# A fused attention and feed-forward kernel on one core: the first phase put in order by a list scheduler

## The chip, the core and the metric

The kernel runs on one core of a Trainium2 chip. The time is the device time of one execution in microseconds (us), from runs of the whole kernel. Five engines take part, each with a queue of its own that it works off in order: TensorE (PE, the matmuls, with the weight loads shown as PEld), VectorE (DVE), ScalarE (ACT), GpSimd (POOL, which does almost nothing here) and SyncE (SP), which issues every DMA. An instruction at the head of a queue waits on semaphores for what it reads, and everything behind it in that queue waits with it.

## The reference

Linear attention with a positive feature map, then a gated feed-forward block on its output:

```python
def phi(x):
    proj = np.einsum('bhsd,df->bhsf', x, w_phi)
    proj = proj - np.max(np.abs(proj), axis=-1, keepdims=True)
    return np.concatenate([np.exp(proj), np.exp(-proj)], axis=-1)
q_p, k_p = (phi(q), phi(k))
kv = np.einsum('bhsf,bhsd->bhfd', k_p, v)
z = np.sum(k_p, axis=2)
num = np.einsum('bhsf,bhfd->bhsd', q_p, kv)
den = np.einsum('bhsf,bhf->bhs', q_p, z)[..., None] + 1e-06
...
gate = 1.0 / (1.0 + np.exp(-(x @ w_gate)))
val = x @ w_val
return gate * val @ w_out
```

There are 8 batches, 8 heads, 576 positions of 64 numbers and 128 features. The feed-forward block ("FF") has 4608 tokens, a width of 512 and a hidden width of 1536, which is cut into 12 slices of 128.

## The kernel before

**Two phases.** The first phase does all of the attention and, between its pieces, the first 4 of the 12 FF slices (JA = 4), whose weights stay in on-chip memory. The second phase (`rest_chunks`) does the other 8 slices in blocks of 512 tokens and adds the partial result of the first phase. The change touches the first phase alone.

**An attention step** handles one pair of heads of one batch; there are 32, counted by i. On PE it has the key projection `pk` (16 matmul records for the two heads, into two PSUM banks, and a small one for the last 64 keys, `pk{i}_2`, into a third), the query projection `pq` in two halves of two banks each, the key-value product `kvz`, its transposition `tp`, the numerators `nm` (two halves) and the denominators `dp`. DVE takes the largest magnitude of the keys (`mx`), subtracts it (`dk`), and from step 10 on adds up the keys' exponentials (`s`, `su`), so that `kvz` has fewer matmuls; of the queries it takes the largest magnitude with transposing instructions (`pm`, `pn`, `mb`) and subtracts it (`d`). ACT does all exponentials (`ek`, `eq`, `d`) and copies out of PSUM. The denominators go through memory (`dn`, `den`, `rb`: three DMAs in a row with a reciprocal on DVE between the first and the second), and DVE multiplies: `xp`, the attention output, which is stored to `xs`. Batch 0 hands its output to the FF directly as well (`xh`, `xl`).

**An FF chunk** is 256 tokens; there are 18, counted by c. Each has 8 halves of 12 matmuls (`gv`: the gate and value products of the 4 slices) and two output blocks of 12 matmuls (`acc`). Behind each pair of halves stand two activations and a cast on ACT (`t`, `u`, `hh`) and four instructions on DVE (`t`, `t`, `u`, `hl`). Every value is kept as a high and a low part, which is why one product takes three matmuls. A chunk can start when the attention of its tokens is stored.

**Weights.** Each of the 12 weight tiles of the first phase is loaded twice (`wraw`, `wmid`) and turned from 64-bit numbers into the two parts by five DVE instructions (`weight_tile`). The second phase does the same (`from_f64`, six DVE instructions a tile) for 24 tiles; 14 of them lie in the last hundred microseconds of the first phase, when the attention's buffers have become free for them.

**The order** in the first phase is what the program text records (`manual_schedule`). The loop over i writes the PE pieces of neighbouring steps in a fixed sequence and calls `fill` four times a step. `fill` puts FF halves and output blocks (`ready`) behind them, at a rate that spreads the FF work of a batch over the steps until the next batch is due. Whatever hangs on a piece is a generator that `tick` moves on by one stage, so that its place on DVE and ACT follows from how many ticks have passed. PSUM banks of the attention come from one pool of 5 (`ps_a`); `gv` has 2 and `acc` 1. Nearly all attention buffers are held twice.

Of the kernel before, what the change touches and what calls it, by code (L numbers as in the profile page):

```python
# [20 lines left out]
F = 128  # L21
P = 128
# [16 lines left out]
RATE = 2.8  # L39
LAG = (4, 8)  # L40
AHEAD = 3
TICKS = 3
# [3 lines left out]
def attention_moe(  # L46
# [63 lines left out]
    def raw_tile(w, sp):  # L110

        j, m = divmod(w, 3)
        raw = sp.tile([P, 2 * DM], U32, tag="wraw", name=f"wraw{j}_{m}")
        nc.sync.dma_start(raw, w_moe[j, :, m, :].bitcast(U32))
        mid = sp.tile([P, 2 * DM], U32, tag="wmid", name=f"wmid{j}_{m}")
        nc.sync.dma_start(
            mid[:, : 2 * DM - 1].bitcast(U16),
            w_moe[j, :, m, :].bitcast(U16)[:, 1 : 4 * DM - 1],
        )
        return raw, mid  # L120

    def weight_tile(w, raw, mid, wp, sp):
        j, m = divmod(w, 3)
        n = f"{j}_{m}"
        if m == 0:
            weights[j] = tuple(
                wp.tile([P, 3 * DM], F32R, tag=f"w{x}{j}", name=f"w{x}{j}") for x in "hl"
            )
        h, l = (x[:, m * DM : m * DM + DM] for x in weights[j])
        hi = raw.rearrange("p (n two) -> p n two", two=2)[:, :, 1]  # L130
        words = mid.rearrange("p (n two) -> p n two", two=2)
        rest, unit = words[:, :, 0], words[:, :, 1]
        top = sp.tile([P, DM], U32, tag="wtop", name="wtop" + n)
        vec.tensor_scalar(top, hi, 0x7FFFFE00, None, op0=ALU.bitwise_and)
        act.activation(top, top, AF.Relu, bias=ebias, scale=8.0)
        vec.tensor_scalar(rest, rest, 0x01FFFFFF, None, op0=ALU.bitwise_and)
        yield
        vec.scalar_tensor_tensor(
            top, hi, 0x80000000, top, op0=ALU.bitwise_and, op1=ALU.bitwise_or
        )  # L140
        nc.sync.dma_start(h.bitcast(U32), top)
        yield
        vec.tensor_scalar(unit, top, 0xFF800000, None, op0=ALU.bitwise_and)
        vec.scalar_tensor_tensor(
            l, rest, 2.0**-36, unit.bitcast(F32), op0=ALU.mult, op1=ALU.mult
        )

# [40 lines left out]

    tasks = []

    def start(g):

        if next(g, tasks) is not tasks:
            tasks.append(g)

    def tick():
        for g in list(tasks):
            if next(g, tasks) is tasks:
                tasks.remove(g)

    def half_units(js, mp, ps_gv, ps_acc, need):
        xs, hs, gvs, parts = {}, {}, {}, collections.Counter()

        def load_x(c):
            xh, xl, raw = x_tiles(mp, CH, f"1_{c}")
            xs[c] = xh, xl
            nc.sync.dma_start(raw, xscr[c])
            for _ in range(3):
                yield
            act.copy(xh, raw)  # L210
            yield
            vec.tensor_tensor(xl, raw, xh.bitcast(F32), op=ALU.subtract)  # L212
            parts[c] = NP

        def begin(c):
            free = c < 2 or parts["v", c - 2] == len(js)
            if c not in xs and free and parts["x", c] == CH * NP:
                start(load_x(c))

        def gate(c, i, n):  # L220
            gv = gvs.pop((c, i))
            u = mp.tile([P, CH], F32, tag="u", name="u" + n)
            t = mp.tile([P, CH], F32, tag="t", name="t" + n)
            hh = mp.tile([P, CH], F32R, tag="hh", name="hh" + n, bufs=10)
            hl = mp.tile([P, CH], F32R, tag="hl", name="hl" + n, bufs=10)
            hs[c, i] = hh, hl, None
            act.activation(t, gv[:, 0, :], AF.Tanh, scale=0.5)
            act.activation(u, gv[:, 0, :], AF.Exp)
            yield
            tu = t.bitcast(U32)  # L230
            vec.tensor_scalar(tu, tu, 0x7FFFFFFF, None, op0=ALU.bitwise_and)
            vec.scalar_tensor_tensor(t, t, 1.0, gv[:, 1, :], op0=ALU.add, op1=ALU.mult)
            vec.scalar_tensor_tensor(u, u, 1.0, t, op0=ALU.min, op1=ALU.mult)
            yield
            act.copy(hh, u)  # L235
            yield
            vec.tensor_tensor(hl, u, hh.bitcast(F32), op=ALU.subtract)  # L237
            parts["h", c] += 1

        def half(c, i, m):  # L240
            while parts[c] < NP:
                begin(c)
                tick()
            need(js[i], m)
            n = f"1_{c}_{js[i]}"
            if m == 0:
                gvs[c, i] = ps_gv.tile([P, 2, CH], F32, tag="gv", name="gv" + n)
            mm_in(gvs[c, i][:, m, :], xs[c], js[i], m, CH)
            if m == 1:
                parts["v", c] += 1  # L250
                start(gate(c, i, n))
                begin(c + 1)

        def half_out(c, t):
            need(js[-1], 2)
            while parts["h", c] < len(js):
                tick()
            acc = ps_acc.tile([P, DM], F32, tag="acc", name=f"acc1_{c}_{t}")
            for i, j in enumerate(js):
                mm_out(acc, t, hs[c, i], j, i == 0, i == len(js) - 1)  # L260
            y = mp.tile([P, DM], F32, tag="y", name=f"y1_{c}_{t}")
            act.activation(y, acc, AF.Copy, scale=0.5)

            def store():
                yield
                nc.sync.dma_start(yscr[c][t], y)

            start(store())

        def unit(c, i):  # L270
            return [(1.45, lambda m=m: half(c, i, m)) for m in range(2)]

        def chunk(c):

            items = []
            for i in range(len(js)):
                items += unit(c, i)
                if i < 2:
                    items += outs(c - 1)[i : i + 1]
            return items  # L280

        def first():

            items = []
            for i in range(len(js)):
                items += unit(0, i) + unit(1, i)
            return items + outs(0)

        def outs(c):
            return [(0.69 * len(js), lambda t=t: half_out(c, t)) for t in range(2)]  # L290

        return chunk, first, outs, begin, xs, parts
# [60 lines left out]
    with ExitStack() as actx:  # L353
# [8 lines left out]

        steps = [(b, p) for b in range(B) for p in range(NP)]
        N = len(steps)

        def bank(shape, name, i=N, ps=None, tag=None):

            if i < EARLY:
                return ps.tile(shape, F32, tag=tag, name=name)
            return ps_a.tile(shape, F32, tag="a", name=name)  # L370
# [106 lines left out]
        def copies(cs):  # L477
            for o, x in cs:
                act.copy(o, x)
# [391 lines left out]
```

## Time and profile before

| | |
|---|---|
| three runs | 1291.21, 1295.24, 1296.06 us (median 1295.24) |
| span of the profiled execution, first to last instruction | 1291.7 us; the profile gives no other time for it |
| first phase, to the first matmul of the second | 694.8 us |
| last transposition of the attention (`tp31`) | 587.2 us |
| PE, DVE, ACT busy in the span | 96%, 61%, 41% |

The profile gives the busy time of each engine in any stretch, the clock that TensorE was granted there (PEclk, 1.00 is full), the single instructions in order of time, and for each idle time the instruction that ended it. Matmuls are pipelined: the time between the starts of two blocks says what a block costs, while a matmul's own duration is longer than that.

### The profile page before, as it was taken

How to read it: one execution, taken by the hardware profiler on the slowest of the kernel's cores; microseconds unless marked ns; L12 is line 12 of the kernel's file. 1: busy time of each engine (PE TensorE's matmuls, PEld its weight loads, DVE VectorE, ACT ScalarE, POOL GpSimd, SP SyncE). 2: the span in 40 equal slices, each digit the busy share in tenths (PEclk: the TensorE clock that was granted, in tenths of full speed). 3: DMA queues.
4: the chain of work that ended last, by engine and by line, in shares of the span. 5: the costliest groups of instructions: out<-in, count | busy, mean ns of one | idle time of the engine just before them, and what ended most of it. 6: DMA issues, size and time to landing. Idle time of an engine off the chain costs nothing.

```text
span 1291.7 us, 22705 instructions
## 1 busy us (share of the span) xinstructions
PE 1234.4 (96%) x9264; PEld 971.2 (75%) x9264; DVE 786.1 (61%) x1584; ACT 528.1 (41%) x1081; POOL 0.7 (0%) x6
## 2 busy tenths in 40 slices
PE   7767999999999999999889999999999999999998
PEld 5434677777777777777778888888888888888886
DVE  6779778888878778883895953434243434333333
ACT  4635556665655566563443422212222212222221
POOL 0000000000000000000000000000000000000000
PEclk8877899999999999999899999999999999999999
DMA  4448434343433334332754520202020111111010
GB/s 176 153 145 284 136 104 146 111 132 105 127 119 121 99 98 146 98 104 73 270 195 148 195 98 1 95 3 76 22 61 37 58 40 53 46 41 57 6 61 33
DMA packets 80868, 131.56 MB, mean 102 GB/s; under 512 B 18300, under 2 KB 37884, under 8 KB 80764
## 3 DMA queue, kind: packets, MB, share of 16 engines
q1 hardware_dynamic: 80764, 130.11, 31.4%
q8 instruction: 73, 1.20, 0.4%
q14 instruction: 31, 0.25, 0.1%
HBM read 92.04 MB, written 28.45 MB: 93 GB/s over the span
## 4 chain that ended last, share of the span: by engine, by line
PE 86%; DVE 7%; DMA 3%; ACT 2%; issue 1%; SPq 0%; DVEq 0%
PE acc L172 22%; PE g L165 15%; PE v L165 15%; PE gv L165 13%; PE kvz L534 6%; PE nm L584 4%; PE pq L417 3%; PE dp L597 2%; PE pk L427 2%; PE kvz L548 1%; DMA wraw<-w_moe 1%; PE pk L488 1%; ACT ek L460 1%; PE tp L560 1%; DMA rb<-den 1%
## 5 line engine op out<-in xcount | busy, mean ns | idle before, releaser
L165 PE MATMUL gv<-xh,wh 128*128 128x256 f32 x576 | 171.6, 298 | 4.9 <-ACT xh L210 2.6
L172 PE MATMUL acc<-wh,hh 128*128 128x512 f32 x432 | 172.4, 399 | 3.2 <-ACT hh L235 2.5
L172 PE MATMUL acc<-wh,hl 128*128 128x512 f32 x432 | 169.0, 391 | 0.7 <-DVE hl L237 0.7
L172 PE MATMUL acc<-wl,hh 128*128 128x512 f32 x432 | 169.1, 391 | 0.0
L165 PE MATMUL gv<-xl,wh 128*128 128x256 f32 x576 | 164.5, 286 | 2.8 <-DVE xl L212 2.8
L165 PE MATMUL gv<-xh,wl 128*128 128x256 f32 x576 | 164.3, 285 | 0.0
L63 ACT CAST hh<-u 128x512 fp32r<-128x512 f32 x72 | 44.7, 621 | 229.0 <-DVE u L186 229.0
L184 DVE TENSOR_SCALAR t<-t 128x512 uint32<-128x512 uint32 x72 | 30.7, 426 | 166.9 <-ACT t L181 166.7
L165 PEld LDWEIGHTS gv<-xh,wh 128*128 128x128 f32 x576 | 111.5, 194 | 22.7 <-issue 15.7
L181 ACT ACTIVATE t<-g 128x512 f32<-128x512 f32 x72 | 43.0, 598 | 178.5 <-PE g L165 178.4
L165 PEld LDWEIGHTS gv<-xl,wh 128*128 128x128 f32 x576 | 111.7, 194 | 3.5 <-DVE xl L212 3.0
L165 PE MATMUL g<-xh,wh 128*128 128x512 f32 x288 | 113.0, 392 | 0.0
L165 PE MATMUL v<-xh,wh 128*128 128x512 f32 x288 | 112.6, 391 | 0.0
L165 PE MATMUL g<-xh,wl 128*128 128x512 f32 x288 | 112.5, 391 | 0.0
L165 PE MATMUL g<-xl,wh 128*128 128x512 f32 x288 | 112.5, 391 | 0.0
L165 PE MATMUL v<-xl,wh 128*128 128x512 f32 x288 | 112.3, 390 | 0.0
L165 PE MATMUL v<-xh,wl 128*128 128x512 f32 x288 | 112.1, 389 | 0.0
L165 PEld LDWEIGHTS gv<-xh,wl 128*128 128x128 f32 x576 | 111.5, 194 | 0.0
L185 DVE SCALAR_TENSOR_TENSOR t<-t,v 128x512 f32<-128x512 f32 x72 | 49.4, 686 | 97.3 <-PE v L165 97.3
L172 PEld LDWEIGHTS acc<-wh,hh 128*128 128x128 f32 x432 | 81.1, 188 | 27.3 <-issue 6.2
L172 PEld LDWEIGHTS acc<-wh,hl 128*128 128x128 f32 x432 | 81.1, 188 | 20.2 <-DVE hl L237 1.7
L534 PE MATMUL kvz<-ek,v 128*32 128x256 f32 x1280 | 89.6, 433 | 6.8 <-issue 5.8
(97 smaller groups left out, 2141.1 us busy)
## 6 DMA issues: line engine op xcount, KB each, us to landing
wraw<-w_moe SPq DMA_DIRECT2D x36, 512.0 KB
xl<-xs SPq DMA_DIRECT2D x34, 512.0 KB
k<-k SPq DMA_DIRECT2D x32, 320.0 KB
v<-v SPq DMA_DIRECT2D x32, 320.0 KB
q<-q SPq DMA_DIRECT2D x32, 288.0 KB
wh<-wtop SPq DMA_DIRECT2D x36, 256.0 KB
ys<-y SPq DMA_DIRECT2D x36, 256.0 KB
yp<-ys SPq DMA_DIRECT2D x36, 256.0 KB
```

What stands on the lines that cost most here:

```text
L63: a = act.copy(h, x)
L165: nc.tensor.matmul(o, a[:, ws], x[:, cs], start=i == 0, stop=i == 11)
L172: nc.tensor.matmul(acc, a[:, ts], w[:, ws], start=first and i == 0, stop=last and i == 2)
L181: act.activation(t, g, AF.Tanh, scale=0.5)
L184: vec.tensor_scalar(tu, tu, 0x7FFFFFFF, None, op0=ALU.bitwise_and)
L185: vec.scalar_tensor_tensor(t, t, 1.0, vl, op0=ALU.add, op1=ALU.mult)
L417: nc.tensor.matmul(pps[hd], wk[head(hd), :], x[head(hd), cs], start=True, stop=True)
L427: nc.tensor.matmul(pps[hd][:, t, :], kx[head(hd), t * P : t * P + P], wk[head(hd), :], start=True, stop=True,)
L460: act.activation(e[:, :, sg * F : sg * F + F], dk, AF.Exp, scale=1.0 - 2.0 * sg)
L534: nc.tensor.matmul(kvz[o : o + Q, : 2 * F], vx[:, 2 * t + hd, o % D : o % D + Q], (e0, e1)[hd][:, t, :] if t < 4 else e2[:, 0, :], start=t ...
L584: nc.tensor.matmul(nms[hf][o : o + Q, :], w[:, sg, o : o + Q], es[sg][:, o // D, cs], start=sg == 0, stop=sg == 1, tile_position=(0, o),)
L597: nc.tensor.matmul(dp[o : o + Q, :], w[:, 2, z : z + Q], es[sg][:, hd, hf * HS : hf * HS + HS], start=sg == 0, stop=sg == 1, tile_position ...
```

## The change

Nothing is computed in another way: the matmuls, the DVE and ACT instructions, the buffers and the DMAs of the first phase are the same in kind and number, and the second phase is untouched. What is new is who sets the order. Every piece of work of the first phase becomes an `Op` with an engine, a modelled duration, a lag, the buffers that it reads and writes, and a rank. `Plan.run` then plays the work through: again and again it takes, for each engine, the operations whose inputs are written, computes when each could start (a buffer of a full ring must first come free), keeps those that could start within SLACK of the earliest, picks the lowest rank among them, and records the one that starts first over all engines. Attention step i has rank 100 i and up; the FF's matmuls have a million and up, so that they are taken only when no attention piece is ready; the gate's instructions on DVE and ACT have ranks below zero and go ahead of all else. The order that comes out is fixed at build time.

```diff
 JR = 8
 EARLY = NP
 ONPE = 10
-RATE = 2.8
-LAG = (4, 8)
-AHEAD = 3
-TICKS = 3
+FRANK = 1e6
+WRANK = 350.0, 420.0, 520.0, 620.0
...
+    def op(self, eng, busy, lag, fn, reads=(), writes=(), rank=0, mode=None):
+        after, bufs = {}, {}
+        for items, wr in ((reads, False), (writes, True)):
+            for it in items:
+                b, part = it if isinstance(it, tuple) else (it, None)
+                bufs[b] = None
+                for o, p, w in b.log:
+                    if (w or wr) and (p is None or part is None or p == part):
...
+    def run(self):
+        free = dict.fromkeys(("PE", "DVE", "ACT", "SP"), 0.0)
...
+                    return None
+                t = max(t, sorted(g.free)[n - 1])
...
+            for e, cs in ready.items():
...
+                t, o = min(
+                    ((t, o) for t, o in ts if t <= first), key=lambda x: (x[1].rank, x[0])
+                )
+                if best is None or t < best[0]:
+                    best = t, o
+            if best is None:
+                raise RuntimeError("no work can go on")
+            t, o = best
+            ready[o.eng].remove(o)
+            for b in o.bufs:
...
+                if not b.left and b.ring:
+                    b.ring.free.append(b.end)
+            for n in o.then:
...
+            order.append((t, o))
+            left -= 1
+            o.fn()
+        return order
...
+        def pe(mode, busy, fn, reads, writes, rank):
+            plan.op("PE", busy, 0.25, fn, reads, writes, rank, mode)
+
+        def dve(n, fn, reads, writes, rank, k=1.0):
+            plan.op("DVE", 0.065 + n / 960 / k, 0.12, fn, reads, writes, rank)
+
+        def on_act(n, fn, reads, writes, rank):
+            plan.op("ACT", 0.09 + n / 1180, 0.12, fn, reads, writes, rank)
+
+        def sp(size, fn, reads, writes, rank):
+            plan.op("SP", 0.06, 2.0 + size / 250e3, fn, reads, writes, rank)
...
+            return buf(ps_a, "a", 5, shape, name)
...
+            pe("r", 0.9, keys, [kx], pk[:2], r + 3)
+            pe("f", 0.25, rest, [kx], pk[2:], r + 4)
...
+            pe("c", 2.16 + (0.36 if su else 0.9), kv, [vx, *ek] + [su] * bool(su), [kvz], r + 17)
...
-            due += min(RATE, sum(c for c, _ in ready) / max(1, left))
-            while ready and due >= ready[0][0] / 2:
-                cost, f = ready.pop(0)
-                f()
-                tick()
-                due -= cost
...
-        for i in range(EARLY, N + 1):
-            load(i + 2)
-            grant(3 * (i - 1))
-            if i + 1 < N:
-                keys(i + 1)
-                copies(q_half(i + 1, 0))
-                fill()
-                copies(q_half(i + 1, 1))
-                rest(i + 1)
-                start(q_max(i + 1))
-                fill()
-            if i < N:
-                kv(i)
-            if i > EARLY:
-                num(i - 1)
-                if i % NP == 0:
-                    queue(i // NP - 1)
...
+            n, r = f"{j}_{m}", WRANK[j] + m
...
+            j, n, r = js[i], f"1_{c}_{js[i]}", FRANK + 10 * c
+            gv = buf(ps_gv, "gv", 2, [P, 2, CH], "gv" + n)
+            for m in range(2):
+                pe(
+                    "f", 1.45,
+                    lambda m=m: mm_in(gv()[:, m, :], [x() for x in xs[c]], j, m, CH),
+                    [*xs[c], wmark[3 * j + m]], [(gv, m)], r,
...
+            g = -100.0 + c
+            on_act(CH, lambda: act.activation(t(), gv()[:, 0, :], AF.Tanh, scale=0.5), [gv], [t], g)
...
+            r, n = FRANK + 10 * c + 12, f"1_{c}_{t}"
...
+        for i in range(N):
+            attend(i)
+            if i < 4:
+                for m in range(3):
+                    weigh(3 * i + m)
+            if i % NP == NP - 1:
+                lo = 0 if i < NP else ((i // NP) * S) // CH
+                for c in range(lo, ((i // NP + 1) * S) // CH):
+                    if c >= 2:
+                        load_x(c)
+                    for u in range(len(js)):
+                        unit(c, u)
+                    for t in range(CH // P):
+                        unit_out(c, t)
+        plan.run()
```

`attend(i)` makes the operations of one step with the same instructions as before; only a few of its lines are shown. An output block counts as one operation of 2.76 us in the plan, an FF half as 1.45 us.

So many FF pieces stand ahead of a transposition in PE's queue (halves and output blocks, of 144 and 36 in all):

| | before | now |
|---|---|---|
| ahead of `tp10` | 18 and 3 | 17 and 2 |
| ahead of `tp31`, the last | 108 and 25 | 65 and 14 |
| behind `tp31` | 36 and 11 | 79 and 22 |

Three places in the queues follow. In the names the first number is the step (`kvz4`, `xp3`) or the chunk and slice (`gv1_0_0`: phase 1, chunk 0, slice 0; `t1_14_1`: chunk 14, slice 1), or slice and part for weights (`wtop1_0`); the last number only counts buffers.

PE, at the first FF matmuls; before:

```order
L548 MATMUL kvz4_1039<-ek4_2_804,halves_130 32x128 x4
L560 MATMUL tp4_1095<-ident_123,kvt4_1080 128x128 x3
L165 MATMUL gv1_0_0_1103<-xh1_0_664,wh0_598 128x256
L165 MATMUL gv1_0_0_1103<-xl1_0_665,wh0_598 128x256
L165 MATMUL gv1_0_0_1103<-xh1_0_664,wl0_599 128x256
```

and now:

```order
L507 MATMUL kvz4_951<-ek4_2_948,halves_130 32x128 x4
L419 MATMUL pk5_2_996<-wk_134,k1_1_606 128x128
L419 MATMUL pk6_2_1004<-wk_134,k1_2_730 128x128
L519 MATMUL tp4_1008<-ident_123,kvt4_998 128x128 x3
L241 MATMUL gv1_0_0_1030<-xh1_0_593,wh0_371 128x256
L241 MATMUL gv1_0_0_1030<-xl1_0_611,wh0_371 128x256
L241 MATMUL gv1_0_0_1030<-xh1_0_593,wl0_372 128x256
```

The FF starts behind `tp4` in both. What moved are the small key projections: `pk5_2` and `pk6_2`, of the next step and of the one after it, now stand ahead of `tp4`, each in a PSUM bank of its own until DVE has read it.

DVE, where batch 0 ends; before:

```order
L519 STREAM_TRANSPOSE mb4_863<-pm4_861 128x1152
L524 TENSOR_TENSOR d4_727<-d4_727,mb4_863 128x1152
L438 TENSOR_REDUCE mx5_0_953<-pk5_0_943 128x4
L438 TENSOR_REDUCE mx5_1_956<-pk5_1_944 128x4
L134 TENSOR_SCALAR wtop0_2_966<-wraw0_2_658 128x512
L136 TENSOR_SCALAR wmid0_2_660<-wmid0_2_660 128x512
L451 TENSOR_TENSOR dk5_0_972<-pk5_0_943,mx5_0_953 128x512
L451 TENSOR_TENSOR dk5_1_974<-pk5_1_944,mx5_1_956 128x512
L138 SCALAR_TENSOR_TENSOR wtop0_2_966<-wraw0_2_658,wtop0_2_966 128x512
L143 TENSOR_SCALAR wmid0_2_660<-wtop0_2_966 128x512
L144 SCALAR_TENSOR_TENSOR wl0_599<-wmid0_2_660 128x512
L638 TENSOR_TENSOR xp2_986<-ex2_805,rb2_838 128x576
```

and now:

```order
L702 TENSOR_TENSOR xl1_0_611<-xp3_1002,xh1_0_593 128x256
L702 TENSOR_TENSOR xl1_1_656<-xp3_1002,xh1_1_596 128x256
L576 STREAM_TRANSPOSE mb4_1043<-pm4_903 128x1152
L584 TENSOR_TENSOR d4_830<-d4_830,mb4_1043 128x1152
L756 TENSOR_SCALAR wtop1_0_1060<-wraw1_0_541 128x512
L765 TENSOR_SCALAR wmid1_0_714<-wmid1_0_714 128x512
L756 TENSOR_SCALAR wtop1_1_1078<-wraw1_1_848 128x512
L765 TENSOR_SCALAR wmid1_1_862<-wmid1_1_862 128x512
L429 TENSOR_REDUCE mx5_0_1083<-pk5_0_938 128x4
L831 TENSOR_SCALAR t1_0_0_1081<-t1_0_0_1081 128x256
L836 SCALAR_TENSOR_TENSOR t1_0_0_1081<-t1_0_0_1081,gv1_0_0_1030 128x256
L843 SCALAR_TENSOR_TENSOR u1_0_0_1085<-u1_0_0_1085,t1_0_0_1081 128x256
```

Before, the last of batch 0's outputs, `xp2`, stands behind the keys of step 5 and a weight tile. Now `xp3` is the last of the four, the FF's first gate (`t1_0_0`, `u1_0_0`) follows fifteen rows behind it, and the weight tiles of slice 1 stand around it.

DVE, where the attention ends; before:

```order
L231 TENSOR_SCALAR t1_14_0_7946<-t1_14_0_7946 128x256
L232 SCALAR_TENSOR_TENSOR t1_14_0_7946<-t1_14_0_7946,gv1_14_0_7917 128x256
L233 SCALAR_TENSOR_TENSOR u1_14_0_7945<-u1_14_0_7945,t1_14_0_7946 128x256
L237 TENSOR_TENSOR hl1_14_0_7948<-u1_14_0_7945,hh1_14_0_7947 128x256
L638 TENSOR_TENSOR xp31_8003<-ex31_7801,rb31_7834 128x576
L231 TENSOR_SCALAR t1_14_1_7998<-t1_14_1_7998 128x256
L232 SCALAR_TENSOR_TENSOR t1_14_1_7998<-t1_14_1_7998,gv1_14_1_7971 128x256
L233 SCALAR_TENSOR_TENSOR u1_14_1_7997<-u1_14_1_7997,t1_14_1_7998 128x256
L237 TENSOR_TENSOR hl1_14_1_8000<-u1_14_1_7997,hh1_14_1_7999 128x256
L81 TENSOR_SCALAR wtop4_0_8709<-wraw4_0_8707 128x512
L83 SCALAR_TENSOR_TENSOR wtop4_0_8709<-wraw4_0_8707,wtop4_0_8709 128x512
L81 TENSOR_SCALAR wtop4_1_8720<-wraw4_1_8718 128x512
```

and now:

```order
L831 TENSOR_SCALAR t1_8_2_6949<-t1_8_2_6949 128x256
L836 SCALAR_TENSOR_TENSOR t1_8_2_6949<-t1_8_2_6949,gv1_8_2_6896 128x256
L843 SCALAR_TENSOR_TENSOR u1_8_2_6951<-u1_8_2_6951,t1_8_2_6949 128x256
L851 TENSOR_TENSOR hl1_8_2_6970<-u1_8_2_6951,hh1_8_2_6968 128x256
L688 TENSOR_TENSOR xp31_6972<-ex31_6849,rb31_6933 128x576
L831 TENSOR_SCALAR t1_8_3_6987<-t1_8_3_6987 128x256
L836 SCALAR_TENSOR_TENSOR t1_8_3_6987<-t1_8_3_6987,gv1_8_3_6936 128x256
L843 SCALAR_TENSOR_TENSOR u1_8_3_6994<-u1_8_3_6994,t1_8_3_6987 128x256
L851 TENSOR_TENSOR hl1_8_3_7001<-u1_8_3_6994,hh1_8_3_6999 128x256
L805 TENSOR_TENSOR xl1_10_6989<-xl1_10_6989,xh1_10_7032 128x1024
L195 TENSOR_SCALAR wtop4_0_8709<-wraw4_0_8707 128x512
L197 SCALAR_TENSOR_TENSOR wtop4_0_8709<-wraw4_0_8707,wtop4_0_8709 128x512
```

The last attention output, `xp31`, stood between the gates of chunk 14; now it stands in those of chunk 8, with chunks 9 to 17 still to come. The second phase's weight tiles (`wtop4_0`) follow right behind it in both.

More of the change, by code (lines that the diff above doesn't have):

```diff
@@ L187, in gated @@
         return hh, hl, split(hh, hl, u)
[L189 to L242, printed above, removed]
-                tick()
[L244 to L292, printed above, removed]
@@ L364, in attention_moe @@
         N = len(steps)
[L366 to L370, printed above, removed]
+        js = list(range(JA))
         ident = at1.tile([P, P], F32, name="ident")
@@ L593, in num, with kv @@
+            kvz = bank([P, 3 * F], f"kvz{i}", early and "acc")
+            def kv():
+                e0, e1, e2 = (e() for e in ek)
+                o_ = kvz()
+                for t in range(5):
                     for o in range(0, P, Q):
                         hd = o // D
-                        hf = n if soon else o // Q % 2
-                        z = (2 * hd + sg) * Q
                         nc.tensor.matmul(
-                            dp[o : o + Q, :], w[:, 2, z : z + Q],
-                            es[sg][:, hd, hf * HS : hf * HS + HS],
-                            start=sg == 0, stop=sg == 1, tile_position=(0, o),
-                        )
@@ new lines, in attend, with turn @@
+            pe("c", 2.16 + (0.36 if su else 0.9), kv, [vx, *ek] + [su] * bool(su), [kvz], r + 17)
+            kvt = buf(at, "kvt", 1, [P, 3 * F], f"kvt{i}")
+            on_act(3 * F, lambda: act.copy(kvt(), kvz()), [kvz], [kvt], r + 18)
+            tp = bank([P, 3, P], f"tp{i}", early and "acc")
+            def turn():
+                for m in range(3):
+                    nc.tensor.transpose(
+                        tp()[:, m, :], kvt()[:, m * F : m * F + F], ident
+                    )
@@ new lines, in den, with go @@
+            def den(soon, n):
+                dp = bank([P, HS], f"dp{i}_{n}", early and "gv")
+                def go():
+                    for sg in range(2):
+                        for o in range(0, P, Q):
+                            hd = o // D
+                            hf = n if soon else o // Q % 2
+                            z = (2 * hd + sg) * Q
+                            nc.tensor.matmul(
+                                dp()[o : o + Q, :], w()[:, 2, z : z + Q],
+                                es[sg]()[:, hd, hf * HS : hf * HS + HS],
+                                start=sg == 0, stop=sg == 1, tile_position=(0, o),
+                            )
+                pe("c", 0.97, go, [w, e, d], [dp], r + 25)
+                return dp
@@ L651, in scale @@
                 )
-                parts[c] += 1
             t = 0
@@ L790, in attention_moe @@
[L790 to L797 removed]
+                wd = min(CH - o, S - t)
+                sp(
+                    wd * 512,
+                    lambda c=c, o=o, t=t, wd=wd: nc.sync.dma_start(
+                        xscr[c][:, p * CH + o : p * CH + o + wd], xp()[:, t : t + wd]
+                    ),
+                    [xp], [(xmark[c], (p, b))], r + 34,
+                )
```

811 lines of the change are left out of this document (452 added, 359 removed).

## Prediction

> **What bounds the kernel now.** I read the page first: how busy each engine is and where PE's clock falls.
>
> ```profile
> span 1291.7 us, 22705 instructions
> ...
> PE 1234.4 (96%) x9264; PEld 971.2 (75%) x9264; DVE 786.1 (61%) x1584; ACT 528.1 (41%) x1081; POOL 0.7 (0%) x6
> ...
> PEclk8877899999999999999899999999999999999999
> ```
>
> PE carries the kernel, but the share is a mean over unlike stretches, and the clock is low in the first five slices. So next the busy time in five stretches: the start, the time in which the feed-forward work (FF) begins, the mixed middle, the end of the first phase, and the second phase.
>
> ```profile
> core 0: us, PE busy (x) PEld busy (x) DVE busy (x) ACT busy (x) POOL busy (x), PEclk, DMA share, GB/s
> 0.00:80.00 80.00, 58.76 (x693) 35.33 (x694) 53.34 (x114) 40.55 (x88) 0.70 (x6) 0.88 0.45 150
> 80.00:160.00 80.00, 62.83 (x675) 41.95 (x674) 69.64 (x151) 39.99 (x85) 0.00 (x0) 0.78 0.64 208
> 160.00:560.00 400.00, 399.16 (x4363) 305.15 (x4363) 325.28 (x718) 242.56 (x546) 0.00 (x0) 1.00 0.39 118
> 560.00:695.00 135.00, 121.14 (x947) 102.61 (x946) 91.95 (x210) 60.52 (x127) 0.00 (x0) 0.95 0.44 148
> 695.00:1292.00 597.00, 592.54 (x2592) 486.20 (x2591) 245.87 (x394) 144.42 (x235) 0.00 (x0) 1.00 0.18 60
> ```
>
> The second phase is dense PE work and stays as it is: 597 us that nothing here can move. Between 160 and 560 PE is busy in all but 0.84 us at full clock, DVE in 81%. What can be won lies before 160 and after 560. What PE waited for there, up to 200 us and then from 580 to 700 us, stands in the list of waits.
>
> ```profile
> PE pq L417 <- ACT d L479: 21.1, 6, 5.2
> PE kvz L534 <- issue: 5.8, 2, 4.7
> PE pk L427 <- DMA k<-k: 4.4, 1, 4.4
> ...
> PE gv L165 <- DVE xl L212: 2.8, 1, 2.8
> PE gv L165 <- ACT xh L210: 2.6, 1, 2.6
> PE acc L172 <- ACT hh L235: 2.5, 3, 1.2
> ```
>
> The six waits of `pq` for ACT's copies are waits for a PSUM bank at the second half of a step's queries, with the whole step behind them in PE's queue. The waits of `gv` near the end are a chunk whose `xh` and `xl` came late.
>
> What a piece costs PE is the distance between starts in the order of time. One step of the middle, in which only the first matmul of each FF half is shown:
>
> ```profile
> 299.98 1.16 PE L427 MATMUL pk<-wk,k 64*128 64x128 f32 x16
> 300.97 0.66 PE L417 MATMUL pq<-q,wk 64*128 64x288 f32 x4
> 301.56 0.39 PE L165 MATMUL gv<-xh,wh 128*128 128x256 f32 x1
> ...
> 303.18 0.76 PE L417 MATMUL pq<-q,wk 64*128 64x288 f32 x4
> 303.87 0.49 PE L488 MATMUL pk<-wk,k 128*128 128x128 f32 x2
> 304.11 0.36 PE L165 MATMUL gv<-xh,wh 128*128 128x256 f32 x1
> ...
> 305.72 2.37 PE L534 MATMUL kvz<-ek,v 128*32 128x256 f32 x40
> ...
> 308.33 0.67 PE L584 MATMUL nm<-eq,kv 128*32 128x288 f32 x8
> ...
> 310.27 0.67 PE L597 MATMUL dp<-eq,kv 128*32 128x288 f32 x8
> ...
> 311.36 0.38 PE L165 MATMUL gv<-xh,wh 128*128 128x256 f32 x1
> ...
> 312.89 0.40 PE L172 MATMUL acc<-wh,hh 128*128 128x512 f32 x1
> ...
> 315.64 0.49 PE L560 MATMUL tp<-ident,kvt 128*128 128x128 f32 x3
> 316.06 0.71 PE L427 MATMUL pk<-wk,k 64*128 64x128 f32 x7
> ```
>
> Keys 0.99, the two query parts 0.59 and 0.69, the small key part 0.24, `kvz` with its sums 2.61, numerators 1.94, denominators 1.09, transposition 0.42: an attention step is 8.57 us. The three FF halves are 1.62, 1.61 and 1.53, so 1.55 is a fair price between attention pieces; an output block is 2.75. Where FF runs alone, the chain of waits has a row of six halves:
>
> ```profile
> 597.74 8.82 PE gv L165 x72
> ```
>
> 1.47 each. Three more rows place the stages: the transpositions of steps 10 and 31, and the first matmul of the second phase.
>
> ```profile
> 210.43 0.49 PE L560 MATMUL tp<-ident,kvt 128*128 128x128 f32 x3
> ...
> 587.23 0.49 PE L560 MATMUL tp<-ident,kvt 128*128 128x128 f32 x3
> ...
> 694.83 0.39 PE L165 MATMUL g<-xh,wh 128*128 128x512 f32 x1
> ```
>
> **The change, stage by stage.** No instruction is added or taken away, so every term is a matter of waiting: I lay out when `tp10`, `tp31` and the first phase's end come, with the counts of FF pieces from the table of the change.
>
> Stage 1, to `tp10`. FF cannot help yet, for it needs batch 0, and the work of DVE ahead of this point is what counts. Step 10's `su`, on which its `kvz` waits, has the same work ahead of it on DVE in both queues (the same eleven steps of keys, twelve weight tiles, eight gates and two pairs of sums; one query chain of 5.7 us less and two `xl` and one `xp` more now), and before it ended at 195.7:
>
> ```profile
> 195.26 0.43 DVE L474 TENSOR_TENSOR su<-s 128x256 f32<-128x256 f32 x1
> ```
>
> By then DVE had been busy 53.3 + 69.6 us and 35.7 us at the middle's 81%, 29: some 152, and idle 44. The 27 us idle in the first 80 are the latency of the first steps, which nobody can fill; I cost the new order of the loads and of the early steps there at nothing, for DVE's first 60 us of work stand in nearly the same sequence. The remaining 99 us of DVE work took 116. With the attention ahead of all else and no fixed number of ticks between its stages they take between 99 (no idle) and 114 (the 87% of the row 80 to 160). I take 107, 93%, between the two: that row has this mix of keys, weights and first gates, but lost part of its time to the order that the change replaces. Then `su` ends at 187 and `tp10` follows `kvz` (2.61) at about 190, 20 us earlier than before, with one FF half and one output block fewer done: 4.3 us of PE. Bounds 182 and 197.
>
> Stage 2, `tp10` to `tp31`. PE has 21 steps x 8.57 = 180.0, 48 halves x 1.55 = 74.4 and 12 blocks x 2.75 = 33.0: 287 us. Before, 90 halves and 22 blocks stood there, and 180.0 + 139.5 + 60.5 = 380 agrees with the measured 376.8, so PE's prices hold. The new thing is DVE's density. Its work in the middle stretch, by groups:
>
> ```profile
> L506 DVE TRANSPOSE_TENSOR_REDUCE pm<-d 128x36 f32<-128x1152 f32 x22 | 30.3, 1378 | 14.4 <-ACT d L479 14.4
> ...
> L233 DVE SCALAR_TENSOR_TENSOR u<-u,t 128x256 f32<-128x256 f32 x46 | 19.6, 425 | 1.6
> L232 DVE SCALAR_TENSOR_TENSOR t<-t,gv 128x256 f32<-128x256 f32 x46 | 19.4, 422 | 6.1
> L237 DVE TENSOR_TENSOR hl<-u,hh 128x256 fp32r<-128x256 f32 x46 | 19.4, 421 | 26.3 <-ACT hh L235 26.1
> ...
> L212 DVE TENSOR_TENSOR xl<-xl,xh 128x1024 fp32r<-128x1024 f32 x11 | 13.4, 1216 | 5.2 <-ACT xh L210 5.0
> L231 DVE TENSOR_SCALAR t<-t 128x256 uint32<-128x256 uint32 x46 | 13.2, 287 | 11.0 <-ACT t L227 10.9
> ```
>
> 22 steps and 46 gates made 325.3 us. Now stage 2 has the same 22 query chains and 24 gates: 22 gates x 1.56 = 34 and five `xl` x 1.2 = 6 fall away, 285 us are left. So 287 us on PE stand beside 285 on DVE, and neither can run at 100% while each waits for the other through the steps. Lower end: 293, DVE at 97%. Upper end: 351, DVE at the 81% of the middle. I take DVE at 94%, 303: the middle's 81% came about because PE set the pace there, so it is no measure of what DVE can do; 87% is the nearest row with DVE in the lead, but half of its hindrance was PE waiting with nothing to fill, and now an FF half is always at hand. `tp31` comes at 190 + 303 = 493, instead of 587.
>
> ACT had 61% in the middle and gets denser, to 61% x 377 / 303 = 76% less the share of 42 fewer halves: no bound by itself. SP carries the same DMAs; in the middle they took 39% of the engines' time, near 50% now, and the three DMAs of the denominators, with `xp` behind them in DVE's queue, are the one place where a slow DMA would show.
>
> Stage 3, to the end of the first phase. Behind `tp31` stand 79 halves x 1.47 = 116.1, 22 blocks x 2.75 = 60.5 and step 31's numerators and denominators, 3.0, with 0.4 for the transposition: 180 us. Before, 36 x 1.47 + 11 x 2.75 + 3.4 = 86.6 took 107.6, so 21 us were waits and low clock. The cause stays: the second phase's first weight tiles follow `xp31` on DVE and in the DMA queue in both, between the gates. It is covered no better now, but the burst is over after some four chunks, and what it delays by then can lie behind the blocks of the chunk before. Ends 0 and 21; I take 11, the middle, since the rows speak for either. The first phase ends at 493 + 180 + 11 = 684 against 694.8.
>
> Sum: 11 us less than the profiled 1291.7, so 1281; the runs' median is 3.5 us above that span, and the same 11 off 1295.2 gives 1284. The 94 us by which the attention ends earlier are mostly FF work put off, not saved: what is won is stage 1's 20 less 4 and stage 3's 10, and stage 2 gives back 16.
>
> **The rivals.**
>
> Denser than I think. Stage 1 at 182, stage 2 in 293 and no waits in stage 3: 655, 40 us less, 1255. For it: DVE's 97% is reached in no row as long as stage 2, but FF halves always stand by. Against: the halves are placed by modelled times, and the queues are fixed.
>
> DVE sets the pace with gaps; this one is slower. PE's `kvz` needs `su` and the exponentials, `pq` needs banks, and behind `tp4` the small key projections of one or two later steps hold banks out of five. Every time DVE or ACT is late by more than the model has it, PE stands at an attention piece with FF behind it in its queue, as in the six waits of 3.5 us for `d`. If DVE keeps 84% in stage 2, this takes 339, and the end is 190 + 339 + 191 = 720: 25 us more, 1320. It decides from 314 us in stage 2 on, 91%, which is not far from my 94.
>
> The clock. Where PE has pauses, it is granted less:
>
> ```profile
> 80.00:90.00 10.00, 5.25 (x40) 2.53 (x42) 9.86 (x19) 2.61 (x6) 0.00 (x0) 0.50 0.51 139
> ```
>
> Half the clock at 52% busy, and in the stretches above 0.78 at 79%, 0.95 at 90% and 1.00 at 99.8%. If stage 2 gets 0.95, its 287 us of PE become 302 and my 16 us of waits come on top: 318, and the first phase ends at 699, 4 us later: 1299. The Trainium skill ("TensorE: Matmul & The Clock Gate", Part 1) says that the clock is gated to half after an idle window of about 3.4 us and released by as long a busy one. By that rule pauses of 1 us between FF halves would cost nothing and only gathered ones count, which gives my forecast and not this rival; the trace agrees as far as its half clock stands where PE waited 4.7 us.
>
> **Chances.** The forecast has 0.50, with a range of its own from 1271 to 1298; denser 0.18; gaps 0.23; clock 0.09. 0.5% of 1295.2 is 6.5 us, about what a measurement can tell from no change: faster is below 1288.7, slower above 1301.7. Of the forecast 0.34 lie below and 0.16 within; denser is all faster; gaps all slower; of the clock 0.06 lie within and 0.03 above. So faster 0.52, same 0.22, slower 0.26. The range, 1256 to 1312, leaves out the outer part of the two ends, about 0.2.
>
> **What would show it.** Right: `tp10` near 190, `tp31` near 493 with DVE over 90% busy in between, PE's clock 1.00 there but for single windows, FF alone behind it with its waits at the second phase's weights, and the first `g` near 684. Wrong: many waits of PE for `su`, `ek`, `d` in stage 2 (gaps), a clock below 0.95 (clock), or `tp10` no earlier than 200, which would say that not the order but a chain of latencies holds the start.

## The result, and the profile after

The changed kernel takes 1342.2 us (median of 4 runs, 1340.9 to 1346.1), the kernel before beside it 1294.5: a ratio of 1.038 (95% interval 1.036 to 1.040). I had forecast 1284 and a range up to 1312. The times of the experiments below are medians of 3 to 12 executions; two slow ones, 4215 us of e5 and 2004 us of e8, are left out of them. The profiled execution has these totals (busy time by engine, and the granted clock in 40 slices):

```profile
span 1339.9 us, 22754 instructions
...
PE 1243.2 (93%) x9264; PEld 974.2 (73%) x9264; DVE 792.2 (59%) x1584; ACT 532.9 (40%) x1081; POOL 0.7 (0%) x6
...
PEclk8898899899999999988999999999999999999999
```

The engines work nearly as long as before (PE 9 us more, DVE 6); the span is 48 us longer. Three rows of the order of time place the stages, `tp10`, `tp31` and the second phase's first matmul:

```profile
194.94 0.55 PE L519 MATMUL tp<-ident,kvt 128*128 128x128 f32 x3
...
537.02 0.49 PE L519 MATMUL tp<-ident,kvt 128*128 128x128 f32 x3
...
743.50 0.39 PE L241 MATMUL g<-xh,wh 128*128 128x512 f32 x1
```

Forecast were 190, 493 and 684. So stage 1 ended 5 us late, stage 2 took 342 in place of 303, stage 3 206.5 in place of 191. The busy time in stages 2 and 3 (columns as in the table by stretches above: start:end, length, then PE, PEld, DVE, ACT, POOL, the clock, DMA):

```profile
194.94:537.02 342.08, 306.30 (x3496) 211.17 (x3495) 282.69 (x607) 205.74 (x445) 0.00 (x0) 0.98 0.38 110
537.02:743.50 206.48, 186.05 (x1265) 169.96 (x1264) 112.59 (x255) 75.11 (x168) 0.00 (x0) 0.95 0.34 112
```

DVE's work in stage 2 is the 283 us that I had counted (285), but it fills 83% and not 94%. What DVE waited for there, and then what PE waited for there:

```profile
DVE xp L688 <- DMA rb<-den: 23.1, 18, 3.6
DVE pm L555 <- ACT d L543: 7.4, 5, 1.8
DVE dn L665 <- DMA dn<-dr: 6.3, 6, 2.3
DVE s L472 <- ACT ek L450: 5.8, 16, 1.6
...
PE nm L604 <- ACT d L543: 22.7, 9, 4.1
PE tp L519 <- DVE dk L439: 3.9, 4, 1.9
```

`xp` waits in 18 of 21 steps for the copies of the denominators, at the head of DVE's queue. Before, the same wait in stage 2 was:

```profile
DVE xp L638 <- DMA rb<-den: 0.2, 1, 0.2
```

One such chain, followed back through what released each piece (start, length):

```profile
452.81 0.18 DVE dn L665
...
453.01 0.23 DVE dn L666
...
453.25 2.65 DMA den<-dn
...
455.92 0.47 SPq L679
...
456.44 1.80 DMA rb<-den
...
459.03 0.74 issue
459.77 0.76 DVE xp L688
```

From the start of the reciprocal (L666) to `xp` 6.8 us pass. In the 22 pairs between 195 and 560 us it is 6.7 on average (5.5 to 8.4). (The row of 1.80 us for `rb` ends before both halves of `rb` have landed: `xp` still waits until 459.77.) The planner has about 5.1 for it: 0.2 + 0.1 for the reciprocal, 0.06 + 2.02 for `den`, 2 x 0.06 + 2.59 for the two `rb`. In the chains of stage 2, read in stretches of 20 us, `den` took 1.4 to 3.9 us (18 rows, median 2.0), `rb`, from the end of its first issue to the landing of both halves, 2.9 to 5.2 (the other 17 rows, median 3.4), and SP was held 0.3 us by the issue of `den` and 1.1 by the two of `rb`. `dn`, ahead of the reciprocal, held it 0.6 where the planner has 0.06: in all, `dn` included, the chain is some 2 us longer than planned. Before, no `xp` between 195 and 560 us came sooner than 7.0 us behind its reciprocal, 9.6 on average.

### The profile page after: what moved, and what is told of

Same layout as the page of the kernel before. It is cut to its first block, busy times and chain, and to the rows that moved or that the text cites. A ratio compares the mean times of both kernels' runs of the same rounds, so it can differ in the third digit from the quotient of the medians.

```text
span 1339.9 us, 22754 instructions
## 1 busy us (share of the span) xinstructions
PE 1243.2 (93%) x9264; PEld 974.2 (73%) x9264; DVE 792.2 (59%) x1584; ACT 532.9 (40%) x1081; POOL 0.7 (0%) x6
## 4 chain that ended last, share of the span: by engine, by line
PE 62%; DVE 17%; DMA 15%; issue 2%; ACT 2%; SPq 2%; DVEq 0%; ACTq 0%
PE acc L248 20%; PE g L241 15%; PE v L241 15%; PE gv L241 8%; DMA rb<-den 6%; DMA den<-dn 4%; DMA wraw<-w_moe 2%; PE nm L604 2%; DVE pm L555 2%; DVE xp L688 1%; DMA dn<-dr 1%; DVE mb L576 1%; DVE dk L439 1%; DVE d L584 1%; DVE mx L429 1%
## 5 line engine op out<-in xcount | busy, mean ns | idle before, releaser
L248 PE MATMUL acc<-wl,hh 128*128 128x512 f32 x432 | 171.8, 398 | 0.0
L241 PEld LDWEIGHTS gv<-xh,wh 128*128 128x128 f32 x576 | 113.6, 197 | 22.2 <-DVE t L836 10.4
L450 ACT ACTIVATE ek<-dk 128x512 f32<-128x512 f32 (+1 forms) x192 | 92.4, 524 | 21.7 <-DVE dk L439 21.4
```

The lines of the kernel that those rows point to most:

```text
L241: nc.tensor.matmul(o, a[:, ws], x[:, cs], start=i == 0, stop=i == 11)
L248: nc.tensor.matmul(acc, a[:, ts], w[:, ws], start=first and i == 0, stop=last and i == 2)
L450: lambda: act.activation(ek[g]()[:, :, sg * F : sg * F + F], dk(), AF.Exp, scale=1.0 - 2.0 * sg,),
```

## The experiments

Theories. **T1**: the planner takes the chain of the denominators as 2 us too short and puts `xp` there; each wait of `xp` holds up all that stands behind it on DVE, and through DVE PE. **T2**: attention ahead of all else is bound by its own latencies and few buffers (strong form), or by an order made for a DVE and an ACT modelled too fast (weak form), whatever `xp` does. **T3**: the rank itself costs. For stage 3, **S1**: the one PSUM bank of the output blocks; **S2**: the second phase's weights on DVE and DMA. All kernels are edits of the changed one, but for the ninth. Stage lengths are between the three marks as above; the last column is `xp`'s wait for `rb` from the start to `tp31`.

| kernel | tp10 | stage 2 | stage 3 | time | ratio to before (95%) | wait |
|---|---|---|---|---|---|---|
| before | 210.4 | 376.8 | 107.6 | 1292 to 1295 | 1 | 1.7 |
| changed | 194.9 | 342.1 | 206.5 | 1342.2 | 1.038 (1.036 to 1.040) | 38.2 |
| e1 no wait of xp | 182.8 | 313.4 | 205.8 | 1297.8 | 1.005 (1.003 to 1.007) | none |
| e2 lag 3 us longer | 200.1 | 303.4 | 199.1 | 1301.2 | 1.006 (1.004 to 1.009) | 12.4 |
| e3 DVE, ACT slower | 217.2 | 353.9 | 149.1 | 1319.7 | 1.022 (1.019 to 1.025) | 54.0 |
| e4 FF by chunks | 233.0 | 482.7 | 104.9 | 1420.5 | 1.100 (1.098 to 1.102) | 42.9 |
| e5 lag 3 us shorter | 216.3 | 361.5 | 210.4 | 1388.1 | 1.075 (1.072 to 1.077) | 68.0 |
| e6 five banks | 193.4 | 345.3 | 198.0 | 1333.3 | 1.033 (1.030 to 1.036) | 40.9 |
| e7 = e2 + e6 | 199.7 | 303.7 | 193.0 | 1295.7 | 1.003 (1.002 to 1.004) | 11.1 |
| e8 = e7, rb + 4 us | 178.9 | 313.9 | 190.6 | 1282.0 | 0.991 (0.990 to 0.993) | none |
| e9 before, xp early | 213.0 | 386.7 | 107.6 | 1307.1 | 1.012 (1.009 to 1.014) | 62.0 |
| e10 = e7, rb + 8 us | 188.7 | 316.4 | 194.1 | 1291.5 | 0.999 (0.997 to 1.000) | none |
| e11 = e8 + e3 | 193.2 | 341.5 | 138.6 | 1272.4 | 0.985 (0.983 to 0.987) | 1.0 |
| e12 = e8, FF spread | 177.6 | 419.9 | 93.8 | 1291.1 | 0.999 (0.998 to 1.000) | none |

**e1, the wait alone.**

```
+        unity = at1.tile([P, S], F32, name="unity")
+        vec.memset(unity, 1e-16)
...
-                S, lambda: vec.tensor_tensor(xp(), ex(), rb(), op=ALU.mult),
+                S, lambda: vec.tensor_tensor(xp(), ex(), unity, op=ALU.mult),
```

> Every queue stays as it is in the changed kernel; only xp is multiplied by a constant tile instead of by rb, so that it no longer waits for the DMAs of the denominators, which still run (the division is left out). Theory T1 (the loss of stage 2 is xp waiting at the head of DVE's queue for the chain dn, den, rb): the 23.1 us of that wait in stage 2 and most of the 44.8 us in the whole phase come back, tp31 falls from 537 to about 512 and the time from 1342 to about 1300 to 1310. Theory T2 (the attention placed ahead of all else is bound by its own latencies and few buffers, so that DVE cannot be denser whatever xp does): other waits take the place, tp31 stays above 528 and the time falls by under 12 us.

1297.8 us, `tp31` at 496.2. With the planned order and all DMAs still there, 44 us go. Between the two profiled executions it is 41.5 us, and 40.8 of them come ahead of `tp31`, where `xp` had waited 38.2 us: there a microsecond of `xp`'s wait costs about a microsecond of the kernel. The 6.6 us that it waited behind `tp31` cost next to nothing, for stage 3 is 0.7 us shorter without them. `tp31` comes earlier than T1 had it (512), since stage 1 loses its share too (12 us). T2's strong form falls. Stage 2 of e1, PE's longest wait there, and a wait of ACT in the changed kernel and in e1:

```profile
182.79:496.21 313.42, 299.36 (x3495) 207.67 (x3494) 281.63 (x608) 205.19 (x445) 0.00 (x0) 1.00 0.40 120
...
PE nm L606 <- ACT d L545: 5.0, 9, 0.8
...
ACT eq L588 <- DVE d L584: 26.9, 15, 4.3
...
ACT eq L590 <- DVE d L586: 14.9, 15, 1.6
```

The same work on DVE in 29 us less, 90%, and PE's clock back at 1.00. The wait of `nm` for `d`, which was 22.7 us, is down to 5.0. This is how `xp`'s wait reached PE: `nm` needs ACT's exponentials of its step, and a PSUM bank that ACT frees by copying a later step's query projection (`d`, L543). Both stand in ACT's queue at or behind `eq`, and `eq` waited for DVE's `d`, 26.9 us in the changed kernel and 14.9 here.

**e2, the planner told longer times for these three DMAs.**

```
-        def sp(size, fn, reads, writes, rank):
-            plan.op("SP", 0.06, 2.0 + size / 250e3, fn, reads, writes, rank)
+        def sp(size, fn, reads, writes, rank, busy=0.06, lag=2.0):
+            plan.op("SP", busy, lag + size / 250e3, fn, reads, writes, rank)
...
-                    [dr], [dn], r + 27,
+                    [dr], [dn], r + 27, 0.5, 2.3,
...
-                    [dn], [dmark], r + 29,
+                    [dn], [dmark], r + 29, 0.5, 2.6,
...
-                        [dmark], [(rb, hd)], r + 30,
+                        [dmark], [(rb, hd)], r + 30, 0.5, 2.4,
```

> The same order rule, but the planner is told what the denominators' DMAs took on the chip: 0.5 us of SP for each issue (0.06 before) and 2.3, 2.6 and 3.0 us until they land (2.0, 2.0, 2.6), so that xp is placed about 3 us later in DVE's queue. T1: the wait of xp for rb falls from 44.8 us to under 12, tp31 near 515, time 1305 to 1320. T2: the wait falls as well but the time does not, 1332 to 1345.

1301.2 us: 41 us come back without anything left out, a little more than T1 had. The new values are no exact copy of the measured ones: the planner now has about 7.4 us from the reciprocal on, where the changed kernel took 6.7 on average. The waits of DVE in its stage 2 (200 to 503.5 us):

```profile
DVE xp L688 <- DMA rb<-den: 3.6, 5, 1.9
DVE dn L665 <- DMA dn<-dr: 1.7, 2, 1.0
```

Stage 2 takes 303 us here, with four FF halves less in it than in the changed kernel, for the plan is another one and not only `xp` has moved. What is left to the forecast of 1284 is stage 1, 10 us late, and stage 3, 8 us.

**e5, the opposite dose.** The same lines with 0.06, 1.0 in all three places.

> The opposite dose of e2: the planner takes the denominators' three DMAs as 1.0 us each shorter than in the changed kernel (1.0, 1.0, 1.6 us), so that xp is placed about 3 us earlier in DVE's queue. T1: each of the 21 steps of stage 2 loses up to 3 us more at xp; the wait for rb there grows from 23 to 50 us or more, tp31 goes from 537 to 560 to 590, time 1365 to 1400. T2: within 10 us of 1342.

1388.1 us, `tp31` at 577.8. The waits of DVE in its stage 2 (216 to 578 us):

```profile
DVE xp L688 <- DMA rb<-den: 41.5, 18, 5.6
DVE dn L665 <- DMA dn<-dr: 14.0, 12, 2.7
```

So the time follows the modelled lag in both directions: 1388, 1342, 1301 for 3 us less, as it was, and 3 us more. `xp`'s wait for `rb` in stage 2 rose less than I expected (41.5, not 50). Its neighbour `dn` waits 14.0 us in place of 6.3, and another 10.9 us of `xp`'s waits are put down to other instructions in the list.

**e9, the same wait in the old order.** In the kernel before, `xp` follows the issue of `rb` by four ticks; here by one:

```
-            for _ in range(4 if i >= EARLY else 2):
+            for _ in range(1 if i >= EARLY else 2):
                 yield
             yield from scale(i, ex, rb)
```

> The kernel before, with one count changed: xp comes one tick behind the issue of rb's DMAs instead of four (steps from the fifth on), some 3 to 4 us earlier in DVE's queue. T1 as a general rule (a wait at the head of DVE's queue for the chain dn, den, rb costs whatever the order): xp's wait for rb in the middle grows from 0.2 us to 40 us or more, and the time from 1292 to 1310 to 1340. T1 with cover (there DVE is busy only 81% and PE has FF in its queue, so that the same wait falls into DVE's own slack): the wait appears, but the time stays below 1302.

1307.1 us, between the two forms. Stage 2 (213 to 600 us) and its wait:

```profile
213.01:599.71 386.70, 380.67 (x4112) 289.60 (x4111) 305.92 (x676) 228.83 (x515) 0.00 (x0) 1.00 0.38 111
...
DVE xp L638 <- DMA rb<-den: 46.3, 20, 4.4
```

60 us more of `xp`'s wait (62.0 less 1.7) cost 14 us: 0.2 us for each, against about 1.0 ahead of `tp31` in the changed kernel. The wait mostly took the place of others: with 46 us of it in stage 2, DVE is idle 81 us there against 72 before, because `hl` waits 8.7 us for `hh` in place of 24.2, and `t` 3.9 for ACT in place of 10.0. PE stays at 98%. In the changed kernel DVE stood idle 59 us in stage 2 and 32 without the wait (e1): there it was the pace, and nothing covered it.

**e3, the other durations.**

```
-            plan.op("DVE", 0.065 + n / 960 / k, 0.12, fn, reads, writes, rank)
+            plan.op("DVE", 0.14 + n / 960 / k, 0.12, fn, reads, writes, rank)
...
-            plan.op("ACT", 0.09 + n / 1180, 0.12, fn, reads, writes, rank)
+            plan.op("ACT", 0.17 + n / 1180, 0.12, fn, reads, writes, rank)
```

> The planner's durations for DVE and ACT are raised by a constant to what the trace has (0.14 for 0.065 us, 0.17 for 0.09 us); DMAs as they were. With these the plan itself puts tp10 at 190 and tp31 at 522, against 157 and 454 with the old ones, while the chip had 195 and 537. T2 in a weak form (the order is made for engines that are 12% too fast, and is out of step everywhere): waits of PE and DVE fall, time 1310 to 1325. T1: xp is still placed by the old latencies but behind slower neighbours, so a part comes back, 1325 to 1338. T2 in its strong form (the attention's own latencies, whatever the numbers): 1335 to 1350, tp31 at 522 or later.

1319.7 us, in the band of T2's weak form, but not by its way: `xp` waits more (54.0 us), and the gain comes from FF. With slower DVE and ACT the plan finds more holes and puts 90 halves and 20 blocks ahead of `tp31`, where the changed kernel has 65 and 14, so that stage 3 takes 149 us. My expectation took the planner's durations to be too short; they were not. Three DVE instructions in a row of the changed kernel:

```profile
457.22 0.68 DVE L429 TENSOR_REDUCE mx<-pk 128x4 f32<-128x512 f32 x1
457.82 0.41 DVE L851 TENSOR_TENSOR hl<-u,hh 128x256 fp32r<-128x256 f32 x1
458.15 0.28 DVE L429 TENSOR_REDUCE mx<-pk 128x1 f32<-128x128 f32 x1
```

They last 0.68 and 0.41 us, but start 0.60 and 0.33 apart, which is what the planner has (0.065 + 512/960 = 0.60 and 0.33): each overlaps the next by 0.08. Over stage 2 the starts lie 0.60 us apart behind `mx` (34 pairs without a pause, median) and 0.33 behind `hl` (23). I had taken the duration of one for the cost in a row. The Trainium skill ("Perfetto Trace Analysis", Optimizing Scalar/DVE Operations) says that about half of an instruction's fixed overhead in the profile, the write's acknowledgement, overlaps with the next instruction. The trace agrees: `mx` lasts 0.15 us longer than 512/960 us, and 0.08 of them lie under the next.

**e4, the rank by chunks.**

```
-            j, n, r = js[i], f"1_{c}_{js[i]}", FRANK + 10 * c
+            j, n, r = js[i], f"1_{c}_{js[i]}", 100.0 * (4 + c * 28 / 18)
...
-            r, n = FRANK + 10 * c + 12, f"1_{c}_{t}"
+            r, n = 100.0 * (4 + (c + 1) * 28 / 18), f"1_{c}_{t}"
```

> FF chunk c gets the rank 100*(4 + 28c/18), its output blocks that of the next chunk: the FF is spread evenly over steps 4 to 31 again, and attention is no longer ranked above all of it. Theory T3 (the rank itself costs: where attention leads, DVE sets the pace and its gaps stand in PE; where FF is spread, PE has work in them): PE over 97% busy in the middle, tp31 at 590 to 620, stage 3 short, time 1285 to 1305. T1 without T3: xp still waits for rb ahead of the gates, and the time stays within 15 us of 1342.

1420.5 us: both expectations missed, and far. Whole chunks now step ahead of the attention at once; the chain of waits has rows such as

```profile
659.50 24.66 PE gv L241 x191
```

25 us of FF in one piece, while the attention stands. What that costs is seen in the busy time from 160 to 560 us, PE 86% at a clock of 0.93:

```profile
160.00:560.00 400.00, 345.56 (x3408) 253.14 (x3404) 257.17 (x557) 197.28 (x429) 0.00 (x0) 0.93 0.30 91
```

**e6 and e7, stage 3.** In the changed kernel PE's waits in stage 3 are these two:

```profile
PE acc L248 <- ACT y L870: 15.4, 5, 7.5
PE gv L241 <- DVE t L836: 5.1, 3, 2.1
```

`y`, the copy that frees the one bank, stands in ACT's queue behind the second phase's Relu, and that behind DVE and its weights:

```profile
589.14 0.72 ACT L196 ACTIVATE wtop<-wtop,ebias 128x512 uint32<-128x512 uint32 x1 [4.77 <-DVE wtop L195]
589.77 0.58 ACT L870 ACTIVATE y<-acc 128x512 f32<-128x512 f32 x1
```

e6 gives the late blocks other banks, e7 is e6 and e2 together:

```
-            acc = buf(ps_acc, "acc", 1, [P, DM], "acc" + n)
+            if c >= 9:
+                acc = buf(ps_a, "a", 5, [P, DM], "acc" + n)
+            else:
+                acc = buf(ps_acc, "acc", 1, [P, DM], "acc" + n)
```

> The changed kernel, with the output blocks of chunks 9 to 17 in PSUM banks of the attention's pool (five, free by then) instead of the one bank of their own; ahead of tp31 nothing changes. Theory S1 (stage 3 loses its 26 us because the second block of a chunk waits in that one bank for ACT's copy y, which stands in ACT's queue behind the Relu of the second phase's weights): the wait of acc for y, 15.4 us, goes, and the time falls to 1324 to 1330. Rival S2 (the burst of the second phase's weights on DVE and DMA sets stage 3, whatever bank the blocks have): the wait moves to gv behind the gates, time 1336 to 1344.

> e2 and e6 together: the denominators' DMAs at their measured times in the plan and the late output blocks in five banks. T1 with S1: e2 had tp31 at 503.5 and waits of acc for y of 14.7 us; without them 1284 to 1290, below the kernel before by 2 to 8 us. T1 with S2: 1296 to 1302.

1333.3 and 1295.7 us: 9 us less than the changed kernel and 5.5 less than e2, between S1 and S2 both times (the second hardly below S2's 1296). PE's waits in e6 behind 500 us:

```profile
PE gv L241 <- DVE t L836: 10.0, 6, 3.6
PE acc L248 <- ACT y L873: 5.7, 1, 5.7
```

Ten of the 15 us at `acc` went, and half of them came back at `gv` behind the gates. The last 5.7 us are those of the 18th output block in PE's order, the second of chunk 8, which the edit leaves in the one bank; it waits 5.7 us in the changed kernel too. No block that got another bank waits any more, so the bank is a part of stage 3's loss. That the burst of weights is the rest is likely, and was not tested by itself. Ahead of `tp31` PE's order is the changed kernel's but for one exchange within a step, and stage 2 is 3 us longer all the same: from one profile each, a difference of 3 us in a stage says nothing.

**e8 and e10, more distance.** As e7, with 6.4 and with 10.4 in place of 2.4 for `rb`.

> e7 with 4 us more for rb in the plan, so that xp stands behind more of DVE's work. If what is left of the waits in the first 200 us (xp 6.8 us for rb in e2, and 5.0 us of pk for k) comes from xp still standing too early, tp10 falls from 200 to about 185 and the time to 1272 to 1280. If a few us too late cost as much as too early (ex, rb and the scratch writes held longer), 1285 to 1300.

> e8 with 4 us more again for rb in the plan (10.4 us where the chip takes about 3). If e8 had the chain fully covered, more distance brings nothing and holds ex, rb and the scratch writes longer: 1280 to 1292. If waits of xp are left that e8's profile does not show as such, 1270 to 1278.

1282.0 us for e8, 0.9% below the kernel before: `tp10` comes at 178.9 and no `xp` waits. With 4 us more the time is 1291.5: `xp` has nothing left to win. (e10's marks in the table are from its longest execution, 1297.4 us.) Whether buffers held longer cost the 9 us, or merely another order, was not separated.

**e11 and e12, the rest of the model and the rank.** e11 is e8 with e3's edit; e12 is e8 with the FF ranked `100.0 * (10 + (c + i / 4) * 28 / 18)`, its blocks `100.0 * (10 + (c + 1 + t / 4) * 28 / 18)`.

> e8 with the planner's DVE and ACT durations as measured (e3's edit). T2 in the weak form (wrong durations put the rest out of step too): the waits of t and pm for ACT, 20.4 and 11.8 us in e8, fall and the time is 1266 to 1277. T1 alone (only the place of xp mattered): 1278 to 1292.

> e8 with the FF ranked half by half against the attention, spread evenly over the steps (chunk c, slice i as step 10 + 28(c + i/4)/18) in place of behind all attention. T3 (attention above FF costs, since DVE sets the pace there): PE over 98% busy from 160 to 560, tp31 at 570 to 600, stage 3 nearly gone, time 1270 to 1282. Rival (attention first is what wins once xp is placed right): the attention is late at the end and little FF is left to cover it, 1290 to 1310.

e11 is the fastest, 1272.4 us, 1.5% below the kernel before. The time is that of T2's weak form, its reason is not: the durations were no truer, and the waits did not fall together (`pm` for `d` rose from 11.8 to 21.5 us, `t` fell from 20.4 to 15.2). Stage 2 holds 69 halves and 16 blocks here in place of e8's 48 and 11, and PE is 99% busy in it:

```profile
193.24:534.78 341.54, 337.71 (x3793) 244.66 (x3792) 292.51 (x642) 220.70 (x482) 0.00 (x0) 1.00 0.40 117
```

e12 came out at 1291.1, at the rival's end: it puts 116 halves and 28 blocks ahead of `tp31`, which comes at 597 as T3 had it, and its stage 3 of 94 us has PE 80% busy at a clock of 0.89:

```profile
597.46:691.30 93.84, 74.67 (x485) 65.04 (x484) 63.75 (x145) 34.12 (x72) 0.00 (x0) 0.89 0.51 175
```

With `xp` in its place the rank does not cost (e8 beats e12). e11, with an amount of FF within the attention between theirs, is faster than both; whether the amount does it was not separated from the rest of its order.

## Why the prediction was wrong, by its own steps

**Stage 1** came out at 194.9, forecast 190 between 182 and 197, and that was luck in part, for its errors lay against each other. DVE's work in the changed kernel up to 80 us and from there to `tp10`:

```profile
0.00:80.00 80.00, 62.72 (x798) 39.34 (x799) 59.84 (x127) 42.08 (x91) 0.70 (x6) 0.90 0.60 191
80.00:194.94 114.94, 95.39 (x1120) 67.28 (x1118) 90.98 (x203) 65.37 (x142) 0.00 (x0) 0.92 0.53 170
```

I had cost the new order of the first steps at nothing, and DVE's idle time there as latency that nobody can fill; but DVE did 59.8 us of work by then, where it had done 53.3 before (65.8 in e1). Behind 80 us I had it 93% busy; it was 79%, and 82% in e1. `xp` waited 15 us here too, and cost 12: without its wait e1 has 182.8, which is 7 us less than my 190.

**The failed step is stage 2's density of DVE**, 94%, 303 us; it was 83%, 342. The amount of work held (DVE 283 us for 285). I named the place, the denominators' DMAs with `xp` behind them, and gave it no price; by e1 it was 29 us of stage 2, and 41 at `tp31`. The other 10 us are not `xp`'s: without any wait of it, e1 and e8 reach 90 and 89%, which is 313 us, at the end of the rival's bound of 314, and what holds DVE at that stays open. That e8, with FF counts within one of the forecast's, has `tp31` at 492.8 and the second phase at 683.4, where I had 493 and 684, is luck: its stage 1 is 11 us shorter than forecast and its stage 2 11 us longer.

Two numbers that would have warned me were there. The change's planner puts the chain at about 5.1 us, and the trace of before never had `xp` less than 7.0 us behind its reciprocal in the middle. The second is where the old order put `xp`, not what the chain took, but it says that 5.1 had never been tried. Some 2 us in each of 21 steps, with DVE on the path, would have been about 40 us for stage 2: the right size, though more than the 29 that came.

On the planner's 2.0 us: the Trainium skill ("DMA: Bandwidth & Descriptors", Anatomy of one DMA) gives a DMA of GpSimd's path about 2.0 us fixed plus its bytes at 436 GB/s; these are SP's. By the Trainium skill's rule, as an estimate, `den` takes 2.0 and one `rb` 2.3. The traced median of `den` agrees (2.0, its issue included). That of the two `rb` is 3.4 from the end of the first issue, with the second issue of 0.5 in it, so some 2.9 for one; the first issue, 0.5, comes on top.

**Stage 3** was taken at 11 us of waits and had 26. I blamed the weights between the gates; e6 and e7 show that part of it (9 and 6 us) was the single bank with `y` behind those weights on ACT. With both mended, e7, e8 and e10 have 193.0, 190.6 and 194.1, against the forecast's 191. Without `xp`'s wait alone (e1), stage 3 stays 15 us too long, and the first phase ends at 702 for 684.

**The rivals.** "DVE sets the pace with gaps" is what happened, near its price (84%, 339 us). Its sign, PE's waits for `d`, was there too; but it was `nm` that stood, hardly ever `pq` (0.7 us), and most of that wait went with `xp`'s in e1. Its 84% was not worked out from any wait, so that it fits is luck. The clock's rival had 0.95 in stage 2; it was 0.98, and 1.00 in e1, so the clock followed the waits and did not make them. "Denser" was not reached in stage 2 (293 us; the shortest is e2's 303) nor in stage 3; its stage 1 of 182 was, by e8 and e12.

## What to carry to other kernels

Where a scheduler fixes the order by modelled times, compare its durations with the traced ones before anything else, first on chains that end at an in-order queue: an operation placed 2 us early stops all that stands behind it. Placing it late was the smaller error here: e8, planned 7 us later than the changed kernel and with the other banks, is 60 us faster, and e10, 4 us later still, loses 9 of them, by the distance or by its other order. What such a wait costs depends on who is on the path: 0.2 us per us where the waiting engine had idle time to put it in, about 1.0 where it set the pace. A priority that makes an engine the bound turns its small waits, which were free, into time.

## What I had not expected of the hardware

A DMA of 4.5 KB to DRAM and its broadcast back have no fixed time: in the chains of the changed kernel's stage 2 `den` took 1.4 to 3.9 us and `rb` 2.9 to 5.2. Each issue of `rb` also held SP for 0.5 us (median), so the second half starts half a microsecond behind the first.
